# Small slot tensors in PSUM, two copies and one low half on VectorE, one low half in two steps

## The chip, the cores and the metric

The kernel runs on one core of one Trainium2 chip. The metric is device time in microseconds of one execution; of the kernel before there are three timed runs, with a median of 481.51 us (480.97 to 481.91). A separate profiled execution gave the trace; it took 479.18 us. The engines are called PE (matrix), PEld (its weight loads), DVE or VectorE, ACT or ScalarE, POOL or GpSimd, and SP (the queue that issues most DMAs).

## The reference, cut to what matters

Attention with pooled keys and values, and behind it a layer of eight experts of which each token uses one or none:

```
k_p, v_p = means of k, v over groups of 8 positions          # 576 -> 72 per head
attn_out = softmax(q @ k_p.T / sqrt(64)) @ v_p                # 8 batches, 8 heads
x = attn_out as (4608 tokens, 512)
do_compute = x @ w_skip > 0
e_idx = argmax(x[do_compute] @ w_gate);  gate = softmax weight of e_idx
out = x;  out[do_compute] += gate * (relu(xc @ w1[e]) @ w2[e])   # e = e_idx of each token
```

## The kernel before, in words

**Attention.** The 4608 tokens are 36 tiles of 128, and the loop `for t in range(NT)` takes one *turn* for each (t = 0 to 35). It is software-pipelined over three tiles. A turn records, among others, in this order: ScalarE copies the turned probabilities of tile t-2 out of PSUM (`pT`), gathers the ends of the last probabilities (`el`), and, in the turn in which a batch begins, copies its turned values (`vT`, in `turned_v`); VectorE normalises tile t-3 (`rc`, `l`, `x`, every third turn or so `lg` as well); PE computes the scores of tile t, VectorE their row minima (`mn`), PE the gate products of a new batch out of `vT`, ScalarE the exponentials (`e`); PE multiplies probabilities with values for tile t-2 (`o<-vb`, `o<-vl`) and turns the probabilities of tile t-1 (`pt<-cfs,e`, `pt<-cfs,el`). Each engine works its instructions strictly in the order in which they were recorded. The PSUM tile `pt` holds two banks; the turned values use part of the second bank, and so does the tail of the turned probabilities. `o` has one buffer of two banks, so the products of tile t-2 wait until VectorE has read those of tile t-3.

**Side work.** Lists (`act`, `dve`, `gps`) hold small jobs with a first and a last turn and are emptied by budget: key sums on VectorE, high halves of the first expert's weights on ScalarE (`high`), and on POOL the sums of values, the indirect writes of the routing table (`table<-pay`), and the low halves of the weights (`low`, weight minus its high half). `later_low` gives POOL its low halves, with the turns of `LOWS`.

**Slots.** Behind the last tile, `slots` turns the token counts into work units: a chain of some fifty VectorE steps on 128x8 tensors, most of which wait for the one before; at its middle `s_col` feeds a PE product (L1072) and `s_coli` an indirect gather by POOL (L1066) that reads rows of the table. Meanwhile PE works at the first expert on the 256 tokens that were picked early (`products`). Then a barrier, and `experts` runs the units; from there PE is busy to the end.

The names that the change touches: `TURNED`, `BESIDE`, `HALVED` are new tables; `turned_v` (L246), `low` (L607), `later_low` (L699), the end of `attention` (L978 to L1000) and the tensors at the head of `slots` (L1010 to L1024).

Of the kernel before, what the change touches and what calls it, by code (L numbers as in the profile page):

```python
# [40 lines left out]
NT = NTOK // 128  # L41
NE, F = 8, 1024
# [116 lines left out]
def attention(tc, nc, q, k, vm, vr, cf, wg, w1, w2, whi, wlo, out, c, pay, offs, table, near, bufs, late, early, mb, fin, cfs):  # L159
    with ExitStack() as ctx:  # L160
# [84 lines left out]

        def turned_v(b, tp):  # L246
            vTs[b] = vT = vp.tile([128, 3, 128], F32, name="vT", bufs=1)
            nc.scalar.activation(vT, tp, AF.Copy)

        def values_in(b, gs=slice(0, 4), by=None):  # L250
            (by or nc.gpsimd.tensor_copy)(vb[b % 2][:, gs, 0:HD], vss[b].rearrange("p (g d) -> p g d", d=HD)[:, gs])
# [343 lines left out]
        def room(cc):  # L595
            return 5 + cc % 3 if cc < 6 else cc - 6
# [4 lines left out]
        def piece(w, cc, i):  # L601
            return w[0][:, cc, i * 512:i * 512 + 512] if cc < 4 else w[1][:, (cc - 4) * 2 + i, :]
# [1 line left out]
        def high(cc, i):  # L604
            nc.scalar.activation(piece(whi, cc, i), stage[:, room(cc), i * 512:i * 512 + 512], AF.Copy)

        def low(cc, i, by=nc.gpsimd):  # L607
            return by.tensor_tensor(piece(wlo, cc, i), stage[:, room(cc), i * 512:i * 512 + 512],
                                    piece(whi, cc, i).bitcast(F32), ALU.subtract)

        def spin(o, times, n):
            for _ in range(times):
# [86 lines left out]
        def later_low(cc, i):  # L699
            if cc * 2 + i > 12:  # L700
                rest.append(lambda v: low(cc, i, v))
            else:
                ready, last = LOWS[min(cc * 2 + i - 6, len(LOWS) - 1)] if cc > 2 else (now["t"] + 1, wload(cc + 3) - 1)
                gps.add(ready, last,
                        1.25, lambda: low(cc, i))

        def adds(b, ready, last):
            first, small = sums(b)
# [269 lines left out]
        late_lows = rest[:2]  # L978
        rest[:2] = []

        def banks():
            o = ps_o.tile([128, 2, 512], F32, name="o")
            products(clock["dve"] + LATER)
            return (y.rearrange("p (i n) -> p i n", i=4) for y in (o[:, 0], ps_s.tile([128, 512], F32, name="sc")))

        fin["hot"] = (flat(kbd[0])[:, 0:PLACED * 128].rearrange("p (j n) -> p j n", j=PLACED),
                      flat(kbd[1])[:, 0:PLACED * 2 * SLOTS].rearrange("p (j i n) -> p j i n", j=PLACED, i=2))
        fin["pos"], fin["pay"] = cfs[:, 128:256], pay[:, NT - PLACED:]
        for wait in slots(tc, nc, c, offs, table, near, bufs, out, fin, ap, banks):
            if wait == "":  # L990
                products(NT * 99.0, 16)
                evacuate()
                busy[0] = False
            elif wait == "lows":
                while waiting:
                    evacuate()
                products(NT * 99.0, 11)
            elif wait == "rows":
                for f in late_lows:
                    f(nc.vector)  # L1000
            elif wait:
# [5 lines left out]
        return held, steps, rest  # L1007


def slots(tc, nc, c, offs, table, near, bufs, out, fin, p, psum):  # L1010

    rows, slot, gate, nti = (fin[n] for n in ("rows", "slot", "gate", "nti"))
    new = lambda name, dt=F32: p.tile([128, NE], dt, name="s_" + name)
    n = new("n"); ni = new("ni", I32); half = new("half", I32); odd = new("odd", I32); units = new("units")
    three = new("three", I32); wide = new("wide", I32); end = new("end"); zero = new("zero"); le = new("le")
    le1 = new("le1"); w = new("w"); more = new("more")
    none = new("none"); kind = new("kind"); own = p.tile([128, NE, NE], F32, name="s_own")
    few = p.tile([128, 1], F32, name="s_few")
    ends, short = new("ends"), new("short")
    both = p.tile([128, 2], F32, name="s_both")  # L1020
    col = p.tile([128, 4], F32, name="s_col")
    coli = p.tile([128, 1], I32, name="s_coli")
    nc.vector.memset(zero, 0.0)
    nc.vector.tensor_tensor(n, offs, c["below"], ALU.subtract)  # L1024
    yield
# [26 lines left out]
    nc.vector.tensor_tensor(w, w, le, ALU.mult)  # L1052
    yield
    nc.vector.tensor_tensor(le, le1, more, ALU.mult)
    nc.vector.tensor_reduce(col[:, 1:2], w, axis=AX.X, op=ALU.add)
    yield
    nc.vector.tensor_reduce(col[:, 0:1], le, axis=AX.X, op=ALU.add)
    nc.vector.tensor_tensor(col[:, 1:2], col[:, 1:2], near["place"], ALU.add)
    yield
    nc.vector.tensor_tensor(col[:, 0:1], col[:, 0:1], c["third"], ALU.add)  # L1060
    yield
    nc.vector.tensor_scalar(col[:, 2:3], col[:, 0:1], 1.0, float(2 * NE * JT), ALU.is_lt, ALU.mult)
    nc.vector.tensor_tensor(col[:, 1:2], col[:, 0:1], col[:, 1:2], ALU.add)
    yield
    nc.vector.tensor_tensor(coli, col[:, 1:2], col[:, 2:3], ALU.add)
# [3 lines left out]
    nc.vector.tensor_tensor(col[:, 3:4], col[:, 1:2], col[:, 2:3], ALU.add)  # L1069
    tp, tr = psum()  # L1070
    of_row = tr[:, 0, 0:SLOTS]
    nc.tensor.matmul(of_row, col[:SLOTS, 3:4].broadcast_to([SLOTS, 128]), c["ident"][:SLOTS, :SLOTS], start=True, stop=True)  # L1072
    yield ""
    at = p.tile([128, 2, PLACED], I32, name="s_at")
    atf = p.tile([128, 2, PLACED], F32, name="s_atf")
# [651 lines left out]
```

## Time and profile before

| what | us |
|---|---|
| median of three runs | 481.51 |
| the profiled execution | 479.18 |
| its span, first to last instruction | 477.3 |
| PE busy / PEld busy | 457.7 / 398.6 |
| VectorE busy | 284.0 |
| ScalarE busy | 234.2 |
| POOL busy | 206.1 |

The busy time of an engine is the time in which it worked at instructions; matrix products overlap, so a PE that is busy need not be at its peak. The span has three parts that read differently: the attention turns to about 136 us, the slot stage to about 167 us, and the expert units behind it. In rows of the timeline the columns are start, duration, engine, line, operation, out<-in with shapes, and count; brackets hold the idle time before a row and what ended it.

### The profile page before, as it was taken

The numbers are of one execution on the slowest core, as the hardware profiler recorded it, in microseconds if no ns is written. First come the engines' busy times: TensorE is split into PE (matmuls) and PEld (weight loads), VectorE is DVE, ScalarE is ACT, GpSimd is POOL, SyncE is SP. The second block draws the span as 40 slices with busy tenths as digits, with TensorE's granted clock in tenths as the row PEclk, the third lists the DMA queues.
The fourth block names the chain that finished last, engine by engine and source line by source line (L and its number), as shares of the span: only waits on it lengthen the run. The fifth ranks groups of instructions, "written<-read, shape, count | busy, mean of one in ns | idle before, by whom it ended". The sixth has DMA issues, their size and how long they took to land. (4 is left out here: it accounts for less than half of the span.)

```text
span 477.3 us, 12494 instructions
## 1 busy us (share of the span) xinstructions
PE 457.7 (96%) x4244; PEld 398.6 (83%) x4245; DVE 284.0 (60%) x659; ACT 234.2 (49%) x614; POOL 206.1 (43%) x271
## 2 busy tenths in 40 slices
PE   8999999998998899999999999999999999999993
PEld 7777777776887698989989898989898989899872
DVE  3678998988889335584746665232326532545662
ACT  4788899999861124463615443121115522434440
POOL 5588379989886330333223034422223322022020
PEclk9999999999999999999999999999999999999997
DMA  8999899966620293575754725112115542324110
GB/s 297 400 402 402 318 379 412 397 211 205 239 70 13 75 313 143 203 253 178 223 192 161 254 97 181 50 38 68 39 63 169 192 132 65 113 107 147 66 44 8
DMA packets 33216, 87.34 MB, mean 183 GB/s; under 512 B 6750, under 2 KB 7262, under 8 KB 31248
## 3 DMA queue, kind: packets, MB, share of 16 engines
q1 hardware_dynamic: 25728, 71.74, 41.9%
q0 software_dynamic: 7440, 14.99, 9.3%
q8 instruction: 27, 0.44, 0.4%
q14 instruction: 21, 0.17, 0.1%
HBM read 72.58 MB, written 20.19 MB: 194 GB/s over the span
## 5 line engine op out<-in xcount | busy, mean ns | idle before, releaser
L1382 PE MATMUL psl<-xhi,w1hi 128*128 128x256 f32 (+3 forms) x352 | 103.5, 294 | 0.3 <-PEq L1157 0.3
L1383 PE MATMUL psl<-xlo,w1hi 128*128 128x256 f32 (+3 forms) x352 | 103.4, 294 | 0.0
L1384 PE MATMUL psl<-xhi,w1lo 128*128 128x256 f32 (+3 forms) x352 | 103.4, 294 | 0.0
L1288 POOL DMA_INDIRECT out<-ring,slot x34 | 36.7, 1080 | 148.6 <-POOLq L1157 136.2
L1507 ACT ACTIVATE hhi<-psl 128x256 fp32r<-128x256 f32 (+3 forms) x88 | 36.3, 412 | 110.5 <-ACTq L1157 109.8
L1580 DVE SCALAR_TENSOR_TENSOR hlo<-psl,hhi 128x256 fp32r<-128x256 f32 (+1 forms) x88 | 38.1, 435 | 59.1 <-DVEq L1157 59.1
L301 ACT ACTIVATE e<-sc,mn 128x72 f32<-128x72 f32 x288 | 65.1, 343 | 9.9 <-DVE mn L296 9.5
L1382 PEld LDWEIGHTS psl<-xhi,w1hi 128*128 128x128 f32 x352 | 66.1, 188 | 1.1 <-issue 0.7
L1383 PEld LDWEIGHTS psl<-xlo,w1hi 128*128 128x128 f32 x352 | 66.1, 188 | 0.4
L1384 PEld LDWEIGHTS psl<-xhi,w1lo 128*128 128x128 f32 x352 | 66.1, 188 | 0.0
L1497 ACT ACTIVATE xhi<-psd 128x512 fp32r<-128x512 f32 x36 | 19.1, 599 | 73.2 <-ACTq L1157 73.2
L1283 POOL DMA_INDIRECT ring<-out,slot x36 | 41.2, 1145 | 19.1 <-issue 14.9
L1557 DVE TENSOR_TENSOR w2lo<-stage,w2hi 128x1024 fp32r<-128x1024 f32 x28 | 34.2, 1225 | 9.5 <-DVEq L1157 9.5
L410 POOL DMA_INDIRECT table<-pay,r_di x33 | 33.1, 1003 | 14.1 <-DVE p_two L437 7.6
L1404 PE MATMUL psf<-w2hi,hhi 128*128 128x512 f32 x96 | 38.1, 397 | 0.0
L1405 PE MATMUL psf<-w2lo,hhi 128*128 128x512 f32 x96 | 37.5, 390 | 0.0
L1406 PE MATMUL psf<-w2hi,hlo 128*128 128x512 f32 x96 | 37.4, 390 | 0.0
L296 DVE TENSOR_REDUCE mn<-sc 128x4 f32<-128x288 f32 x72 | 30.7, 453 | 11.2 <-PE sc L288 7.2
L1282 POOL COPY ring<-gate 128x1 f32<-128x1 f32 x33 | 8.2, 249 | 63.2 <-DMA out<-ring,slot 55.6
L1557 DVE TENSOR_TENSOR w1lo<-stage,w1hi 128x1024 fp32r<-128x1024 f32 x28 | 32.4, 1220 | 3.4 <-DVEq L1157 3.3
L1405 PE MATMUL mb<-w2lo,hhi 128*128 128x512 f32 x88 | 34.3, 390 | 0.0
L1404 PE MATMUL mb<-w2hi,hhi 128*128 128x512 f32 x88 | 34.3, 390 | 0.0
(293 smaller groups left out, 963.5 us busy)
## 6 DMA issues: line engine op xcount, KB each, us to landing
stage<-in_w SPq DMA_DIRECT2D x64, 512.0 KB, 4.7
out<-x SPq DMA_DIRECT2D x36, 256.0 KB, 7.0
stage<-in_k SPq DMA_DIRECT2D x7, 1152.0 KB
qt<-in_q SPq DMA_DIRECT2D x9, 512.0 KB, 9.9
hlo<-in_vm SPq DMA_DIRECT2D x4, 1024.0 KB, 9.0
hhi<-in_vm SPq DMA_DIRECT2D x4, 1024.0 KB
xhi<-in_q SPq DMA_DIRECT2D x4, 512.0 KB, 7.9
xlo<-in_q SPq DMA_DIRECT2D x4, 512.0 KB, 8.0
```

The lines of the kernel that those rows point to most:

```text
L301: nc.scalar.activation(e[:, g, hh * SP:(hh + 1) * SP], sc[:, h * SP:(h + 1) * SP], AF.Exp, bias=mn[:, 4 * i + h:4 * i + h + 1], scale=-1.0)
L1283: g.indirect_dma_start(ring[:, s % 6, 0:D], None, out, bass.IndirectOffsetOnAxis(ap=slot[:, s:s + 1], axis=0), bounds_check=NTOK - 1, oob_ ...
L1288: g.indirect_dma_start(out, bass.IndirectOffsetOnAxis(ap=offsets, axis=0), ring[:, s % 6, 0:D], None, bounds_check=NTOK - 1, oob_is_err=Fa ...
L1382: t.matmul(ps, whi[0][:, k, w], xhi[:, k, xs], start=(k == 0), stop=False)
L1383: t.matmul(ps, whi[0][:, k, w], xlo[:, k, xs], start=False, stop=False)
L1384: last = t.matmul(ps, wlo[0][:, k, w], xhi[:, k, xs], start=False, stop=(k == 3))
L1404: t.matmul(ps, hhi[:, k, sl], whi[1][:, k, :], start=(k == 0), stop=False)
L1405: t.matmul(ps, hhi[:, k, sl], wlo[1][:, k, :], start=False, stop=False)
L1406: last = t.matmul(ps, hlo[:, k, sl], whi[1][:, k, :], start=False, stop=(k == 7))
L1507: a.activation(hhi[:, f, xs], psL[f % 3][:, xs], AF.Relu).then_inc(sem["act"], 1)
L1557: v.tensor_tensor(chunk_of(wlo, c), chunk_view(stage[c], c), chunk_of(whi, c).bitcast(F32), ALU.subtract).then_inc(sem["wlo"], 1)
L1580: return v.scalar_tensor_tensor(out[:, f, :], psL[f % 3][:, xs], 0.0, hhi[:, f, xs].bitcast(F32), ALU.max, ALU.subtract)
```

## The change

Four edits.

1. Most small tensors of `slots` become columns of a bank of PSUM: `o[:, 1]`, the second bank of the attention's output tile, which is taken before `slots` begins. `zero`, `own`, `le`, `more`, `odd`, `wide` and a few others stay in SBUF; each step then has one SBUF tensor among its inputs at most.
2. `turned_v` copies the turned values of batches 4 and 6 with VectorE, of the others with ScalarE as before. These two copies stand in turns 18 and 27 of the loop's counter (PE turned the values at the end of turns 17 and 26).
3. The low half (4, 0), one of the 128x512 steps on `w2lo`, goes from POOL to VectorE, in turn 32 (`NT - 4`).
4. POOL makes the low half (5, 1) in two steps of 256 columns.

```
+TURNED = 4, 6
+BESIDE = 4, 0, NT - 4
+HALVED = 5, 1
...
         def turned_v(b, tp):
             vTs[b] = vT = vp.tile([128, 3, 128], F32, name="vT", bufs=1)
-            nc.scalar.activation(vT, tp, AF.Copy)
+            if b in TURNED:
+                nc.vector.tensor_copy(vT, tp)
+            else:
+                nc.scalar.activation(vT, tp, AF.Copy)
...
         def later_low(cc, i):
             if cc * 2 + i > 12:
                 rest.append(lambda v: low(cc, i, v))
+            elif (cc, i) == BESIDE[:2]:
+                dve.add(BESIDE[2], BESIDE[2], 0.7, lambda: low(cc, i, nc.vector))
             else:
...
-                gps.add(ready, last,
-                        1.25, lambda: low(cc, i))
+                parts = [slice(0, 256), slice(256, 512)] if (cc, i) == HALVED else [slice(0, 512)]
+                for part in parts:
+                    gps.add(ready, last, 1.25 / len(parts), lambda part=part: low(cc, i, nc.gpsimd, part))
...
+        o = ps_o.tile([128, 2, 512], F32, name="o")
+
         def banks():
-            o = ps_o.tile([128, 2, 512], F32, name="o")
...
-        for wait in slots(tc, nc, c, offs, table, near, bufs, out, fin, ap, banks):
+        for wait in slots(tc, nc, c, offs, table, near, bufs, out, fin, ap, o[:, 1], banks):
...
+    def new(cols=NE, dt=F32):
+        y = beside[:, taken[0]:taken[0] + cols]
+        taken[0] += cols
+        return y if dt == F32 else y.bitcast(dt)
+
+    n = new(); units = new(); end = new(); le1 = new(); w = new(); none = new(); sums = new(3)
+    ni = new(dt=I32); half = new(dt=I32); three = new(dt=I32)
```

VectorE's order around the head of turn 18, before; `kp` is the last step of turn 17, `rc`, `l`, `x` normalise tile 15, `mn` are the minima of tile 18; what an instruction waits for stands in brackets:

```order
L197 TENSOR_REDUCE kp<-stage 128x72 [waits DMAHW1_49]
L344 RECIPROCAL rc<-o 128x8 [waits PE_49]
L348 TENSOR_TENSOR l_1422<-o,rc 128x2x4x9 [waits DVE_49]
L349 TENSOR_TENSOR x<-o,rc 128x2x4x64 [waits DMAHW0_49]
L296 TENSOR_REDUCE mn<-sc 128x4 [waits PE_49,Activation_49]
L296 TENSOR_REDUCE mn<-sc 128x4 [waits PE_49]
```

And the same place now:

```order
L200 TENSOR_REDUCE kp<-stage 128x72 [waits DMAHW1_49]
L252 COPY vT<-pt 128x384 [waits Activation_49]
L350 RECIPROCAL rc<-o 128x8
L354 TENSOR_TENSOR l_1422<-o,rc 128x2x4x9 [waits DVE_49]
L355 TENSOR_TENSOR x<-o,rc 128x2x4x64 [waits DMAHW0_49]
L302 TENSOR_REDUCE mn<-sc 128x4 [waits PE_49] x2
```

The copy stands ahead of tile 15's normalising, and it waits for ScalarE: the value that it waits for is that of the `pT` copy of the same turn, which reads the same bank of `pt`. In turn 27 it is the same, with `lg` between `x` and `mn`.

VectorE's order at the head of `slots`, before:

```order
L1030 TENSOR_TENSOR s_ni<-s_n,nskip 128x8 [waits DVE_49]
L1032 TENSOR_SCALAR s_half<-s_ni 128x8 [waits DVE_49]
L1033 TENSOR_SCALAR s_odd<-s_ni 128x8
L1035 TENSOR_TENSOR s_units<-s_half,s_odd 128x8 [waits DVE_49]
L1036 TENSOR_TENSOR s_three<-s_half,s_odd 128x8
L1039 TENSOR_SCALAR s_none<-s_units 128x8 [waits DVE_49]
L1040 TENSOR_SCALAR s_units<-s_units 128x8 [waits DVE_49]
L1042 SCALAR_TENSOR_TENSOR s_end<-s_units,s_zero 128x8 [waits DVE_49]
L1043 TENSOR_SCALAR s_w<-s_units 128x8
L1044 SCALAR_TENSOR_TENSOR s_more<-s_three,s_odd 128x8
L1045 SCALAR_TENSOR_TENSOR s_more<-s_none,s_more 128x8 [waits DVE_49]
```

And now (`o` is the bank that holds the small tensors; L1055 is the scan, as L1042 was):

```order
L1043 TENSOR_TENSOR o<-o,nskip 128x8 [waits DVE_49]
L1045 TENSOR_SCALAR o<-o 128x8 [waits DVE_49]
L1046 TENSOR_SCALAR s_odd<-o 128x8 [waits DVE_49]
L1048 TENSOR_TENSOR o<-o,s_odd 128x8 [waits DVE_49]
L1049 TENSOR_TENSOR o<-o,s_odd 128x8 [waits DVE_49]
L1052 TENSOR_SCALAR o<-o 128x8 [waits DVE_49]
L1053 TENSOR_SCALAR o<-o 128x8 [waits DVE_49]
L1055 SCALAR_TENSOR_TENSOR o<-o,s_zero 128x8 [waits DVE_49]
L1056 TENSOR_SCALAR o<-o 128x8 [waits DVE_49]
L1057 SCALAR_TENSOR_TENSOR s_more<-o,s_odd 128x8 [waits DVE_49]
L1058 SCALAR_TENSOR_TENSOR s_more<-o,s_more 128x8 [waits DVE_49]
```

The steps and their order are the same, but in one bank of PSUM nearly each waits for the one before it, where four of these eleven had no wait of their own.

POOL's order up to the gather of the table's rows, before:

```order
L608 TENSOR_TENSOR w2lo<-stage,w2hi 128x512 [waits Activation_49]
L410 DMA table<-pay,r_di 36864x8 [waits DMASW0_49]
L410 DMA table<-pay,r_di 36864x8 [waits DMASW1_49]
L608 TENSOR_TENSOR w2lo<-stage,w2hi 128x512 [waits DMAHW2_49,Activation_49]
L410 DMA table<-pay,r_di 36864x8 [waits DMASW2_49,DVE_49]
L410 DMA table<-pay,r_di 36864x8 [waits DMASW3_49]
L1066 DMA stage<-table,s_coli 81x1024 [waits DMASW3_49,DMASW4_49,DVE_49,Pool_49]
```

And now:

```order
L614 TENSOR_TENSOR w2lo<-stage,w2hi 128x256 [waits Activation_49]
L416 DMA table<-pay,r_di 36864x8 [waits DMASW7_49]
L416 DMA table<-pay,r_di 36864x8 [waits DMASW0_49]
L614 TENSOR_TENSOR w2lo<-stage,w2hi 128x256
L416 DMA table<-pay,r_di 36864x8 [waits DMASW1_49]
L416 DMA table<-pay,r_di 36864x8 [waits DMASW2_49,DVE_49]
L614 TENSOR_TENSOR w2lo<-stage,w2hi 128x512 [waits DMAHW2_49,Activation_49]
L416 DMA table<-pay,r_di 36864x8 [waits DMASW3_49]
L1079 DMA stage<-table,s_coli 81x1024 [waits DMASW3_49,DMASW4_49,DVE_49,Pool_49]
```

One 128x512 step of five is gone, one is two of 256, and one write of the table comes behind the last low half instead of two. PE's and SP's instructions stand in the same order as before.

## Rows read from the trace of the kernel before

**Rows 1.** Windows: length, busy PE, PEld, DVE, ACT, POOL; clock, DMA share, GB/s.
```profile
60.00:80.00 20.00, 19.43 (x374) 15.31 (x375) 17.45 (x44) 18.87 (x71) 16.66 (x23) 1.00 1.03 393
...
320.00:340.00 20.00, 20.00 (x136) 18.43 (x136) 6.02 (x12) 3.88 (x10) 5.88 (x9) 1.00 0.16 51
```

**Rows 2.** Timeline of ScalarE in turn 18: start us, duration us, instruction.
```profile
71.54 0.70 ACT L317 ACTIVATE pT<-pt 128x640 f32<-128x640 f32 x1
...
72.42 0.47 ACT L248 ACTIVATE vT<-pt 128x384 f32<-128x384 f32 x1
...
73.31 1.80 ACT L301 ACTIVATE e<-sc,mn 128x72 f32<-128x72 f32 x8
75.37 0.70 ACT L317 ACTIVATE pT<-pt 128x640 f32<-128x640 f32 x1 [0.27 <-PE pt L313]
```

**Rows 3.** Timeline of VectorE in turn 18.
```profile
70.17 0.21 DVE L344 RECIPROCAL rc<-o 128x8 f32<-128x8 f32 x1
...
70.56 0.68 DVE L349 TENSOR_TENSOR x<-o,rc 128x512 f32<-128x512 f32 x1
72.43 0.88 DVE L296 TENSOR_REDUCE mn<-sc 128x4 f32<-128x288 f32 x2 [1.19 <-PE sc L288]
```

**Rows 4.** Timeline of PE in turn 18: values of tile 16, last turned probabilities.
```profile
73.31 0.29 PE L328 MATMUL o<-vb,pT 64*64 64x74 f32 x2
...
75.06 0.27 PE L313 MATMUL pt<-cfs,el 128*128 128x128 f32 x1
```

**Rows 5.** Timeline of VectorE in turns 27 and 28.
```profile
101.36 0.53 DVE L353 TENSOR_REDUCE lg<-l 128x27 f32<-128x216 f32 x1
102.44 0.88 DVE L296 TENSOR_REDUCE mn<-sc 128x4 f32<-128x288 f32 x2 [0.54 <-PE sc L288]
103.65 0.20 DVE L264 COPY vb<-mb 128x36 f32<-128x36 f32 x1 [0.34 <-PE mb L261]
...
106.61 0.81 DVE L296 TENSOR_REDUCE mn<-sc 128x4 f32<-128x288 f32 x2
```

**Rows 6.** Timeline of ScalarE in turns 27 and 28.
```profile
101.55 0.71 ACT L317 ACTIVATE pT<-pt 128x640 f32<-128x640 f32 x1
...
107.09 1.80 ACT L301 ACTIVATE e<-sc,mn 128x72 f32<-128x72 f32 x8 [0.24 <-DVE mn L296]
```

**Rows 7.** Timeline of PE, then of ScalarE, around the head of turn 31.
```profile
115.57 0.44 PE L242 MATMUL pt<-cfs,vs 128*128 128x128 f32 x2 [0.40 <-POOL vs L219]
...
116.21 0.70 ACT L317 ACTIVATE pT<-pt 128x640 f32<-128x640 f32 x1 [0.27 <-PE pt L243]
```

**Rows 8.** Timeline of VectorE, then of POOL, in turn 32.
```profile
122.23 0.21 DVE L344 RECIPROCAL rc<-o 128x8 f32<-128x8 f32 x1 [0.75 <-PE o L330]
...
122.97 1.28 POOL L608 TENSOR_TENSOR w1lo<-stage,w1hi 128x512 fp32r<-128x512 f32 x1
```

**Rows 9.** Timeline of VectorE, of PE and of POOL in the slot chain.
```profile
141.76 0.17 DVE L1024 TENSOR_TENSOR s_n<-offs,cfs 128x8 f32<-128x8 f32 x1
...
143.71 1.99 DVE L1042 TENSOR_TENSOR_SCAN s_end<-s_units,s_zero 128x8 f32<-128x8 f32 x1
...
147.58 0.15 DVE L1069 TENSOR_TENSOR s_col<-s_col 128x1 f32<-128x1 f32 x1
...
147.87 0.42 PE L1072 MATMUL sc<-cfs,s_col 81*128 81x81 f32 x2 [1.29 <-DVE s_col L1069]
...
144.35 1.30 POOL L608 TENSOR_TENSOR w2lo<-stage,w2hi 128x512 fp32r<-128x512 f32 x1
```

**Rows 10.** Timeline of VectorE in turn 30: dependent steps, the first into PSUM.
```profile
114.97 0.16 DVE L481 COPY mb<-p_last 128x1 f32<-128x1 f32 x1
115.17 0.17 DVE L483 TENSOR_SCALAR norder<-mb 128x8 int32<-128x8 f32 x1
```

**Rows 11.** Windows of one microsecond in the slot stage.
```profile
152.00:153.00 1.00, 1.00 (x6) 0.82 (x5) 0.96 (x9) 0.00 (x0) 1.00 (x3) 1.00 0.30 33
```

**Rows 12.** Timeline of POOL: the gather of the table's rows.
```profile
150.25 1.07 POOL L1066 DMA_INDIRECT stage<-table,s_coli x1 [2.15 <-DVE kbd L1083]
```

More of the change, by code (lines that the diff above doesn't have):

```diff
@@ L605, in high, with low @@
             nc.scalar.activation(piece(whi, cc, i), stage[:, room(cc), i * 512:i * 512 + 512], AF.Copy)
-        def low(cc, i, by=nc.gpsimd):
-            return by.tensor_tensor(piece(wlo, cc, i), stage[:, room(cc), i * 512:i * 512 + 512],
-                                    piece(whi, cc, i).bitcast(F32), ALU.subtract)
+        def low(cc, i, by=nc.gpsimd, part=slice(0, 512)):
+            return by.tensor_tensor(piece(wlo, cc, i)[:, part], stage[:, room(cc), i * 512:i * 512 + 512][:, part],
+                                    piece(whi, cc, i)[:, part].bitcast(F32), ALU.subtract)
         def spin(o, times, n):
@@ L1007, in attention, with slots @@
         return held, steps, rest
-def slots(tc, nc, c, offs, table, near, bufs, out, fin, p, psum):
+def slots(tc, nc, c, offs, table, near, bufs, out, fin, p, beside, psum):
     rows, slot, gate, nti = (fin[n] for n in ("rows", "slot", "gate", "nti"))
[L1013 to L1022, printed above, removed]
+    taken = [0]
+    def new(cols=NE, dt=F32):
[4 more added lines that the diff above has]
+    ni = new(dt=I32); half = new(dt=I32); three = new(dt=I32)
+    kept = lambda name, dt=F32, *size: p.tile([128, *(size or (NE,))], dt, name="s_" + name)
+    own = kept("own", F32, NE, NE); zero = kept("zero"); le = kept("le"); more = kept("more"); kind = kept("kind")
+    ends = kept("ends"); short = kept("short"); few = kept("few", F32, 1); odd = kept("odd", I32); wide = kept("wide", I32)
+    both = kept("both", F32, 2); col = kept("col", F32, 3); coli = kept("coli", I32, 1)
     nc.vector.memset(zero, 0.0)
@@ L1054, in slots @@
     nc.vector.tensor_tensor(le, le1, more, ALU.mult)
-    nc.vector.tensor_reduce(col[:, 1:2], w, axis=AX.X, op=ALU.add)
+    nc.vector.tensor_reduce(sums[:, 1:2], w, axis=AX.X, op=ALU.add)
     yield
-    nc.vector.tensor_reduce(col[:, 0:1], le, axis=AX.X, op=ALU.add)
-    nc.vector.tensor_tensor(col[:, 1:2], col[:, 1:2], near["place"], ALU.add)
+    nc.vector.tensor_reduce(sums[:, 0:1], le, axis=AX.X, op=ALU.add)
+    nc.vector.tensor_tensor(col[:, 0:1], sums[:, 1:2], near["place"], ALU.add)
     yield
-    nc.vector.tensor_tensor(col[:, 0:1], col[:, 0:1], c["third"], ALU.add)
+    nc.vector.tensor_tensor(sums[:, 0:1], sums[:, 0:1], c["third"], ALU.add)
     yield
-    nc.vector.tensor_scalar(col[:, 2:3], col[:, 0:1], 1.0, float(2 * NE * JT), ALU.is_lt, ALU.mult)
-    nc.vector.tensor_tensor(col[:, 1:2], col[:, 0:1], col[:, 1:2], ALU.add)
+    nc.vector.tensor_scalar(col[:, 1:2], sums[:, 0:1], 1.0, float(2 * NE * JT), ALU.is_lt, ALU.mult)
+    nc.vector.tensor_tensor(sums[:, 2:3], sums[:, 0:1], col[:, 0:1], ALU.add)
     yield
-    nc.vector.tensor_tensor(coli, col[:, 1:2], col[:, 2:3], ALU.add)
+    nc.vector.tensor_tensor(coli, sums[:, 2:3], col[:, 1:2], ALU.add)
     nc.gpsimd.indirect_dma_start(rows, None, table.rearrange("(r l) t -> r (l t)", l=128),
@@ L1068, in slots @@
                                  bounds_check=NE * JT - 1, oob_is_err=False)
-    nc.vector.tensor_tensor(col[:, 3:4], col[:, 1:2], col[:, 2:3], ALU.add)
+    nc.vector.tensor_tensor(col[:, 2:3], sums[:, 2:3], col[:, 1:2], ALU.add)
     tp, tr = psum()
     of_row = tr[:, 0, 0:SLOTS]
-    nc.tensor.matmul(of_row, col[:SLOTS, 3:4].broadcast_to([SLOTS, 128]), c["ident"][:SLOTS, :SLOTS], start=True, stop=True)
+    nc.tensor.matmul(of_row, col[:SLOTS, 2:3].broadcast_to([SLOTS, 128]), c["ident"][:SLOTS, :SLOTS], start=True, stop=True)
     yield ""
```

## The prediction

> **What bounds the kernel now.** I read the windows first, then the timelines of single engines where an edit lands, and in them the idle times and what ended them. The windows show two regimes [rows 1]. From about 180 us on PE is busy without a gap (20.00 of 20 us), all others far less: that part keeps its length and only moves with its start. In the attention turns no engine is full and none is free: in 20 us ScalarE works 18.87, VectorE 17.45, POOL 16.66. There the turn's chain decides: pT on ScalarE, then values and transposes on PE, then the next pT, and beside it scores, minima on VectorE, exponentials on ScalarE. What an edit is worth is read from who waits last in its turn. Between the two lies the slot stage, with VectorE's chain of small steps, for which PE waits 1.29 us once [rows 9].
>
> **The two copies on VectorE.** Removed from ScalarE: one copy of 0.47 us in each of two turns [rows 2]. Added to VectorE: the same copy, whose price I do not see. Below lies ScalarE's 0.47 for the same 384 columns, above VectorE's own step over 512 columns of PSUM, 0.68 [rows 2, 3]; I take 0.55, since a VectorE step over three quarters of those columns should take somewhat less than that. What counts more is what is queued behind it. VectorE works in order, the copy waits for the pT of its own turn, and rc, l, x and the minima stand behind it.
>
> Turn 18, before: rc started at 70.17 and x ended at 71.24, while VectorE would have waited anyway; the minima started at 72.43, as soon as the scores were there [rows 3]. Now nothing of this starts before pT ends, 71.54 + 0.70 = 72.24 [rows 2]. Copy 0.55, then the block from rc to x, 71.24 - 70.17 = 1.07: x ends at 73.86 and the minima start at about 73.8 (neighbours overlap by some hundredths), 1.4 later than before. The first of two is done after half of 0.88, so the exponentials start at 74.25 instead of 73.31, and end 1.80 later, at 76.05. On PE the values of tile 16 must wait for x, which reads the same buffer: 73.9 instead of 73.31. From their start to the end of the turned probabilities PE took 75.06 + 0.27 - 73.31 = 2.02 [rows 4], so these end at 75.9. The next pT, at 75.37 before, starts at 75.95 to 76.05: plus 0.6. What ScalarE saves is in this already, since it had waited 0.27 for PE there.
>
> Turn 27 is worse, since behind it VectorE has no slack. pT ends at 101.55 + 0.71 = 102.26 [rows 6]; copy 0.55, block 1.07, lg 0.53 [rows 5]: the minima start at about 104.3 instead of 102.44, plus 1.85. Of this 0.34 falls into VectorE's wait for PE before vb, and some 0.1 into overlaps; from 103.65 to the minima of turn 28 at 106.61 VectorE shows no idle time, so these come 1.4 later [rows 5]. The exponentials of turn 28 had waited 0.24 for just these minima [rows 6]: they come 1.4 later too.
>
> Taken up again is little: at the head of turn 31 PE waited for POOL's sums, which do not move, and ScalarE waited 0.27 for PE behind it [rows 7]. So the end of attention comes 0.6 + 1.4 - 0.3 = 1.7 us later. Bounds: 0.6 if only one of the two delays gets through, 2.1 if nothing is taken up and a copy costs 0.68.
>
> **The slot chain in PSUM.** From the first step to the last one ahead of PE's product it takes 147.58 - 141.76 = 5.82 us, of it 1.99 for one scan over 8 columns, where others of that size take 0.17 [rows 9]. The scan ends with POOL's 128x512 step, 144.35 + 1.30 = 145.65 [rows 9]; I read this as a wait for POOL. With its tensors in PSUM I set the scan at 0.2. The other steps lose. Their 26 spacings took 5.82 - 1.99 = 3.83, 0.15 on average, since several steps had no wait of their own. By the order 23 of the 26 now wait for the step before. A dependent step over a result in PSUM follows after 115.17 - 114.97 = 0.20 [rows 10]. So 23 x 0.20 and three of about 0.1, 4.9, and the scan's 0.2: 5.1, and with 0.2 for steps over 64 columns or with a pointer operand 5.3, which is 0.5 less than before. PE's wait of 1.29 covers this gain whole, so it reaches the path. Bounds: 0.9 less with a scan that costs nothing, 1.1 more with a scan that stays at 1.99 (4.9 + 1.99 = 6.9).
>
> [...]
>
> **POOL's part.** VectorE's low half in turn 32 costs it about 0.6 to 0.7 us (x of 512 columns: 0.68 [rows 3]). It stands where VectorE was idle for 0.75, waiting for PE's values [rows 8]; so covered I take it as nothing. Without the cover it is up to 0.7, and more in the second rival. POOL loses a step of 1.30 [rows 9]; the two halves cost no less than one step and at most as much again as a step, I take 0.2. Its last writes and the gather, at 150.25 before [rows 12], can come about 1.1 earlier. This gains nothing by itself: no row of PE shows a wait for the gather, and VectorE's chain, which also feeds it, comes later by now. I take 0, with bounds of -0.3 and 0.2.
>
> **Sum.** 1.7 - 0.5 + 0 + 0 = 1.2 us later, against the profiled execution 479.18 (span 477.3 and 1.88 around it) 480.4. The median of the runs shown lies 2.33 above that execution; I add the difference to the median: 481.51 + 1.2 = 482.7.
>
> **Rivals.**
>
> *The low half in turn 32 is held by POOL.* It reads two tensors of SBUF. In turn 32, shifted by 1.7, it would start at about 123.1, into POOL's step from 122.97 to 124.25 [rows 8]. If it is held until that ends, it is done at 124.9 instead of 123.7; rc, due at 122.23 + 1.7 = 123.9, comes 0.9 later, and with it x, PE's values and the following minima. Then the sum is 2.1, 483.6. For it: the scan's end with POOL's step [rows 9]. Against it: from 152 to 153 us VectorE ran nine short steps, several with two SBUF tensors, while POOL was busy for the whole microsecond [rows 11]. [...]
>
> *The copies gain.* If turns 18 and 27 were set by ScalarE's sum of work, each would shrink by the 0.47 that it gives up [rows 2]. With the slot chain, 2 x 0.47 + 0.5 = 1.4 less: 480.1. It decides if the first minima are ready before ScalarE is, at 73.31 - 0.47 = 72.84 in turn 18. For it: ScalarE is the busiest engine of the turns [rows 1]. Against it: the minima cannot start before x, and x not before the copy; this needs VectorE to be out of its order.
>
> *The chain gets longer.* The scan costs 2.0 by itself, and the added waits stay: 6.9 instead of 5.82, so PSUM brings the chain nothing, and the sum is 1.7 + 1.1 = 2.8: 484.3. For it: the scan started 0.64 before POOL's step that it is said to have waited for. Against it: the end, to within 0.05 us.
>
> *Only part of the delay gets through*, for instance turn 27's alone runs into slack that I did not see between turns 28 and 35: 0.6 - 0.5 = 0.1, 481.6.
>
> **How the numbers follow.** Forecast 0.45, low half held 0.20, longer chain 0.08, partial delay 0.16, copies gain 0.11. The forecast's own range is 481.9 to 483.5, from a delay of 1.4 to 2.1 and a gain of 0.1 to 0.9. About 0.2% of 481.5, or 0.96 us, is what a measurement of this kernel can tell from no change, so the band is 480.55 to 482.47. Slower: 0.72 of the forecast, all of the second and third: 0.32 + 0.28 = 0.60. Within: the rest of the forecast and nearly all of the partial delay, 0.13 + 0.16 = 0.29. Faster: 0.11. Range: up to 484.2, just short of the longer chain, and down to 480.8, where most of the gaining case is left out.
>
> **What would show it.** In the profile after, VectorE should be idle for about 2 us ahead of vT in turns 18 and 27, with ScalarE as what ended it; the minima of these turns should start 1.4 and 1.8 us later, and the first step of the slot chain some 1.7 us later, at about 143.5. The scan should take about 0.2 us and the chain 5.3, with PE's wait at its product near 0.8. The low half in turn 32 should take 0.7 us; with 1.2 or more it was held. If the slot chain's first step comes no later than 141.8, the forecast is wrong at its first and largest term; if the scan keeps its 2 us, at its second.

## The result, and where the time went

The changed kernel is slower by 3.7 us: a median of 484.64 us over 21 runs (479.79 to 490.90), against 480.97 us over 21 runs of the kernel before on the same chips. The ratio is 1.0077, with a 95% interval of 1.0056 to 1.0098. That lies above the range of the prediction. Medians are over all executions, ratios and intervals over those that did not run in a slower state, so the two need not agree. The profiled execution took 485.65 us, its span 483.8, so it stands 6.5 us over the profiled one of before (479.18, span 477.3), and more has to be accounted for in the pair of traces than in the medians.

A ruler for the attention turns is the start of ScalarE's pT at the head of each turn, read from the timelines of the two profiles:

| head of turn | before | after | later by |
|---|---|---|---|
| 9 | 41.55 | 41.17 | -0.38 |
| 13 | 55.59 | 57.55 | +1.96 |
| 18 | 71.54 | 73.49 | +1.95 |
| 19 | 75.37 | 77.89 | +2.52 |
| 27 | 101.55 | 104.02 | +2.47 |
| 30 | 112.35 | 116.08 | +3.73 |
| 31 | 116.21 | 120.83 | +4.62 |
| 33 | 122.94 | 127.55 | +4.61 |
| 34 | 125.80 | 130.92 | +5.12 |

The start is 0.4 us earlier, and the loss comes in six pieces: 2.3 us between turns 9 and 13, 0.6 in turn 18, 1.3 from turn 27 to 30, 0.9 in turn 30, 0.5 from turn 32 (it shows between the heads of turns 33 and 34), and then 1.2 at the slots (below).

The first piece stands ahead of anything that was changed. In the timeline of PE of the profile after, two rows wait for nothing that the profile shows, in the middle of a run of matmuls:

```profile
44.08 0.42 PE L334 MATMUL o<-vb,pT 64*64 64x74 f32 x12 [0.44 <-issue]
...
52.20 0.66 PE L336 MATMUL o<-vl,pT 64*64 64x296 f32 x2 [1.44 <-issue]
```

Five kernels that lack a part of the change will show the same stall, two of them in one profile and not in another, so it is counted here as no part of the change; its cause is open. Without it the pair differs by about 4.2 us, close to the medians.

Turns 18 and 27 went as forecast. VectorE after, in turn 18 and then turn 27:

```profile
74.22 0.56 DVE L252 COPY vT<-pt 128x384 f32<-128x384 f32 x1 [2.03 <-ACT pT L323]
74.70 0.20 DVE L350 RECIPROCAL rc<-o 128x8 f32<-128x8 f32 x1
...
75.08 0.68 DVE L355 TENSOR_TENSOR x<-o,rc 128x512 f32<-128x512 f32 x1
75.68 0.81 DVE L302 TENSOR_REDUCE mn<-sc 128x4 f32<-128x288 f32 x2
...
104.75 0.56 DVE L252 COPY vT<-pt 128x384 f32<-128x384 f32 x1 [2.07 <-ACT pT L323]
...
106.66 0.82 DVE L302 TENSOR_REDUCE mn<-sc 128x4 f32<-128x288 f32 x2
```

VectorE stands still for 2 us ahead of each copy, and rc, x and the minima that had filled that time [rows 3, 5] come after it. ScalarE pays: its exponentials in turn 18 now wait 1.17 us for the minima.

```profile
76.16 1.80 ACT L307 ACTIVATE e<-sc,mn 128x72 f32<-128x72 f32 x8 [1.17 <-DVE mn L302]
77.89 0.70 ACT L323 ACTIVATE pT<-pt 128x640 f32<-128x640 f32 x1
```

The next three pieces were not forecast, or only as a rival. They are one thing in three places: a VectorE step is *held*, that is, it takes far longer than the same step elsewhere and ends only with a step of POOL. VectorE and POOL after, at turn 30, in turn 32 and at the slots' first step; then PE's two waits:

```profile
115.53 1.36 DVE L474 TENSOR_TENSOR mb<-offs,p_apart 128x8 f32<-128x8 f32 x1
...
126.02 1.43 DVE L614 TENSOR_TENSOR w2lo<-stage,w2hi 128x512 fp32r<-128x512 f32 x1
...
146.86 1.89 DVE L1037 TENSOR_TENSOR o<-offs,cfs 128x8 f32<-128x8 f32 x1
...
150.75 0.18 DVE L1055 TENSOR_TENSOR_SCAN o<-o,s_zero 128x8 f32<-128x8 f32 x1
...
153.90 0.15 DVE L1082 TENSOR_TENSOR s_col<-o,s_col 128x1 f32<-128x1 f32 x1
...
115.57 1.27 POOL L222 TENSOR_TENSOR hhi<-hhi 128x512 f32<-128x512 f32 x1
...
125.62 1.27 POOL L614 TENSOR_TENSOR w1lo<-stage,w1hi 128x512 fp32r<-128x512 f32 x1
...
147.39 1.32 POOL L614 TENSOR_TENSOR w2lo<-stage,w2hi 128x512 fp32r<-128x512 f32 x1
...
117.77 0.44 PE L334 MATMUL o<-vb,pT 64*64 64x74 f32 x13 [0.74 <-DVE p_few L476]
...
154.20 0.42 PE L1085 MATMUL sc<-cfs,s_col 81*128 81x81 f32 x2 [2.51 <-DVE s_col L1082]
```

Three VectorE steps with two inputs in SBUF are held: one ends at 116.89 where POOL's sums end at 116.84, one at 148.75 where POOL's low half ends at 148.71, and the low half at 127.45, 0.56 us after POOL's end at 126.89 (0.68 is what it takes where it is not held). The 8-column sum of offs and p_apart had taken 0.15 before. The scan, which was held before [rows 9], now takes 0.18; its hold went to the chain's first step, so the chain takes 153.90 - 146.86 = 7.04 us from its first step to its last, 5.82 before, and PE waits 2.51 in place of 1.29.

### The profile page after: what moved, and what is told of

Its sections match the earlier page's. It is cut to its first block, busy times and chain, and to the rows that moved or that the text cites. A ratio compares the mean times of both kernels' runs of the same rounds, so it can differ in the third digit from the quotient of the medians.

```text
span 483.8 us, 12491 instructions
## 1 busy us (share of the span) xinstructions
PE 458.7 (95%) x4244; PEld 398.8 (82%) x4245; DVE 287.7 (59%) x662; ACT 233.1 (48%) x612; POOL 203.6 (42%) x271
## 5 line engine op out<-in xcount | busy, mean ns | idle before, releaser
L1301 POOL DMA_INDIRECT out<-ring,slot x34 | 35.5, 1045 | 153.1 <-POOLq L1170 140.9
L1419 PE MATMUL mb<-w2hi,hlo 128*128 128x512 f32 x88 | 34.3, 390 | 0.0
```

Of the source, the lines that this page charges most:

```text
L1301: g.indirect_dma_start(out, bass.IndirectOffsetOnAxis(ap=offsets, axis=0), ring[:, s % 6, 0:D], None, bounds_check=NTOK - 1, oob_is_err=Fa ...
L1419: last = t.matmul(ps, hlo[:, k, sl], whi[1][:, k, :], start=False, stop=(k == 7))
```

## Experiments

Theory A: a copy that must wait for pT stops VectorE in order, so VectorE slips against POOL; and a VectorE step with two SBUF inputs is held wherever it meets a POOL step of that kind. Theory B, in its several forms: each edit costs by itself. The expectations give its form for each run. Ratios are to the kernel before, run on the same chip, with 95% intervals; 0.0021 is 1 us.

**One part at a time.** First the copies alone:

```diff
+            if b in TURNED:
+                nc.vector.tensor_copy(vT, tp)
+            else:
                 nc.scalar.activation(vT, tp, AF.Copy)
```

> The kernel before with only the two copies of turned values on VectorE (batches 4 and 6). Theory A (VectorE waits in order for its own turn's pT, and the turns behind it slip into a POOL step): VectorE stands idle about 2 us ahead of each of the two copies; the step from pT to pT grows by 0.6 us in turn 18 and by 1.2 us in turns 27 and 28, and in turn 30 the small product of offs and p_apart takes about 1.3 us in place of 0.15, because it now falls beside POOL's 512-column sums, for another 0.9 us; the slots' chain keeps its 5.8 us. Sum +2.7: about 483.7 us. Theory B (the copies cost next to nothing and the loss is that of the slots and the low half): within 0.3 us of the kernel before, 481.0 us, pT to pT unchanged in both turns.

Measured: 481.33 us, ratio 1.0032 (0.9990 to 1.0074); in the profile the end of attention comes 2.5 us later than before, 2.8 counted from the first turn. Turn 18 grows by 0.57, turns 27 to 29 by 1.25, turn 30 by 1.1. Its rows of VectorE, POOL and PE in turn 30:

```profile
113.25 1.56 DVE L472 TENSOR_TENSOR mb<-offs,p_apart 128x8 f32<-128x8 f32 x1
...
113.50 1.27 POOL L220 TENSOR_TENSOR hhi<-hhi 128x512 f32<-128x512 f32 x1
...
115.69 0.75 PE L332 MATMUL o<-vb,pT 64*64 64x74 f32 x32 [0.95 <-DVE p_few L474]
```

By the trace A's 2.7 us was right to 0.1. The times alone allow -0.5 to 3.6 us. So the hold in turn 30 follows from the copies; it is not in the code that was changed. At the slots the first step was held (1.90) in place of the scan (0.18), with all tensors in SBUF: the chain took 5.7 us and PE waited 1.19, no more than before.

Then the slots' tensors alone, the changed kernel with its other two parts switched off:

```diff
-TURNED = 4, 6
-BESIDE = 4, 0, NT - 4
-HALVED = 5, 1
+TURNED = ()
+BESIDE = 99, 0, NT - 4
+HALVED = 99, 1
```

> The kernel before with only the slots' small tensors in PSUM. Theory A: POOL's 512-column step stands 2.6 us behind the chain's first step as before, where every step now has at most one SBUF input, so the scan takes 0.2 us and no other step is held; the chain is 5.3 us (5.8 before), PE waits 0.8 us in place of 1.3, time -0.5 us: about 480.5 us. Theory B (small steps in PSUM are themselves slower, or are held all the same): the chain is 6.5 to 7 us, PE waits 2 to 2.5 us, about 482.2 us.

Measured: 479.68 us, ratio 0.9980 (0.9941 to 1.0018). The chain is 5.3 us, the scan 0.18, PE's wait 0.78: A, and the forecast's own term of -0.5. The first step stood 2.5 us ahead of POOL's step and took 0.17. By itself this part does what it should; B, slower by 1 us or more, is excluded.

The low halves alone, the kernel before with the changed later_low and low:

```diff
+BESIDE = 4, 0, NT - 4
+HALVED = 5, 1
```

> The kernel before with only the low half of turn 32 on VectorE and the other one made in two steps. Theory A: the low half falls into VectorE's idle time beside POOL's descriptor writing and takes 0.7 us, nothing is late behind it; POOL's last 512-column step now stands 0.5 us behind the chain's first step in place of 2.6, so the first step of the chain (two SBUF inputs) takes 1.9 us and the scan 0.2: the chain stays at 5.8 us and the time within 0.3 us of 481.0 us. Theory B (the low half on VectorE is held by POOL wherever it stands): it takes 1.4 us and the time is +0.5 to +0.9 us, about 481.7 us.

Measured: 484.43 us, ratio 1.0048 (0.9997 to 1.0100), too wide to tell. The profiled run took 478.97. In it the low half took 0.73 beside a DMA_INDIRECT of POOL of 1.03 us (the expectation calls it descriptor writing), and nothing was late behind it. My expectation for the chain was wrong: POOL's last low half stayed 2.5 us behind the first step (144.22 against 141.69), and the scan was held again (2.00). So POOL's new order by itself does not bring the two together: in the changed kernel the first step comes 5.2 us later than here, POOL's step only 3.2. A second profile of this kernel:

> The kernel with only the low halves moved, once more, for a second profile, since half of its times lay near 485 us. Theory A: the scan or another step of the slots' chain is held for some 1.8 us as before, the low half takes 0.7 us, and what is longer than the kernel before is a stall of PE that the profile gives no reason for. Theory B: the low half or the chain is held for 1 us or more beyond that.

It took 487.28 us with the low half at 0.68 and the scan at 2.00, and a first step held for 0.64 by POOL's half step. 4.9 us of it is one wait of PE in the experts' loop, at 220 us, long after the change, which was 0.5 in the first profile; the mean granted clock was 0.96 from 140 to 180 us, with PE's wait of 1.77 us at the slots, and 0.97 from 180 to 240, where the kernel before had 1.00 in both. The low half by itself was not held in either.

**One input of the chain's first step moved.** The changed kernel, with the constant of that step in PSUM:

```diff
+        o = ps_o.tile([128, 2, 512], F32, name="o")
+        nc.vector.tensor_copy(o[:, 1, 248:256], c["below"])
         add_routes(NT)
...
-    nc.vector.tensor_tensor(n, offs, c["below"], ALU.subtract)
+    nc.vector.tensor_tensor(n, offs, beside[:, 248:256], ALU.subtract)
```

> The changed kernel with one more edit: the constant that the chain's first step subtracts is copied into PSUM ahead of the last tiles' routes, so that this step has one SBUF input too. Theory A (the step is held for POOL's 512-column step since it has two SBUF inputs): the first step takes 0.2 us in place of 1.9, the chain 5.3 us in place of 7.0, PE's wait before the product 0.8 us in place of 2.5: -1.6 us against the changed kernel, about 483.0 us. Theory B (whatever step comes there is held, or the first step waits for something else): another step of the chain takes about 1.9 us, the chain stays at 7.0 us and the time at 484.6 us.

Measured: 483.62 us, ratio 1.0056 (1.0025 to 1.0087), where A said 483.0 and B 484.6. The time does not tell them apart: +1.2 to +4.2 us holds both, and this profile had a PE stall of 1.74 us at 102. The trace does. VectorE, POOL and PE at the slots; last, from the run *shift* below, the same VectorE step with both inputs in SBUF, and the POOL step that it met:

```profile
145.29 0.17 DVE L1037 TENSOR_TENSOR o<-offs,o 128x8 f32<-128x8 f32 x1
...
144.39 1.31 POOL L614 TENSOR_TENSOR w2lo<-stage,w2hi 128x512 fp32r<-128x512 f32 x1
...
150.90 0.42 PE L1085 MATMUL sc<-cfs,s_col 81*128 81x81 f32 x2 [0.78 <-DVE s_col L1082]
...
147.43 0.43 DVE L1030 TENSOR_TENSOR s_n<-offs,cfs 128x8 f32<-128x8 f32 x1
...
146.51 1.32 POOL L611 TENSOR_TENSOR w2lo<-stage,w2hi 128x512 fp32r<-128x512 f32 x1
```

The step starts 0.90 us into POOL's and takes 0.17; PE's wait falls from 2.51 to 0.78. In *shift* it starts 0.92 us into POOL's, and takes 0.43, to POOL's end. With one input in SBUF the step was not held here. Nor was one with two in the stretch of rows 11, in the kernel before:

```profile
152.58 0.15 DVE L1098 TENSOR_TENSOR s_none<-s_none,s_odd 128x8 f32<-128x8 f32 x1
...
151.38 1.90 POOL L1081 TENSOR_SCALAR kbd<-cfs,s_atf 128x128 f32<-128x128 f32 x3
```

There a VectorE step with two SBUF tensors took 0.15 us beside POOL's steps of one SBUF tensor with a scalar. So, one misfit below apart, only POOL's two-tensor steps are seen to hold in the traces read here.

**The copies in another place.** The copies alone, each behind the normalising:

```diff
-            if new:
+            if new and new not in TURNED:
                 turned_v(new, tp)
             if t > 2:
                 normal(t - 3)
+            if new in TURNED:
+                turned_v(new, tp)
```

> The kernel with only the two copies on VectorE, and there each stands behind the normalising of three turns before in place of ahead of it. Theory A (the loss in turns 18 and 27 is VectorE standing still, in order, behind a copy that has to wait for pT): VectorE does rc, l and x in those 2 us, the minima are late by 0.6 us at most, the step from pT to pT grows by at most 0.3 us in turn 18 and 0.4 us in turns 27 and 28 together (0.6 and 1.2 with the copy ahead). The slip at turn 30 is then under 1 us, and the small product of offs and p_apart is held less or not at all. About +0.5 us against the kernel before: 480.7 us by its 480.2 us of the last comparison. Theory B (a copy out of this bank on VectorE costs its time wherever it stands): the growth of 0.6 and 1.2 us stays, about 482 us.

Measured: 479.50 us, ratio 0.9989 (0.9959 to 1.0018). VectorE in turn 18, then the product of turn 30:

```profile
71.94 0.21 DVE L348 RECIPROCAL rc<-o 128x8 f32<-128x8 f32 x1
...
72.33 0.68 DVE L353 TENSOR_TENSOR x<-o,rc 128x512 f32<-128x512 f32 x1
...
74.04 0.56 DVE L250 COPY vT<-pt 128x384 f32<-128x384 f32 x1 [1.02 <-ACT pT L321]
74.51 0.81 DVE L300 TENSOR_REDUCE mn<-sc 128x4 f32<-128x288 f32 x2
...
113.45 0.15 DVE L472 TENSOR_TENSOR mb<-offs,p_apart 128x8 f32<-128x8 f32 x1
```

The same copy of 0.56 us now costs nothing: turns 18 and 27 are each 0.06 us shorter than before. The place cost the 1.8 us, not the copy. The changed kernel with this one edit:

> The changed kernel with one more edit: in turns 18 and 27 the copy on VectorE stands behind the normalising of three turns before. Theory A (the copies' place makes VectorE slip, and the slip makes it meet POOL in turns 30 and 32 and at the slots' first step): pT to pT grows by 0 to 0.1 us in turns 18, 27 and 28, the product of offs and p_apart takes 0.15 us, the low half 0.7 us; POOL's 512-column step again stands some 2.5 us behind the chain's first step, which takes 0.2 us, so the chain is 5.4 us and PE waits 0.8 us. Time -0.5 us against the kernel before: about 479.6 us by its 480.0 us. Theory B (the slots' tensors or the low half lose by themselves): only 1.8 us of the loss goes, about 482.5 us.

Measured: 480.24 us, ratio 0.9980 (0.9955 to 1.0004). The product takes 0.15, the low half 0.68. B is excluded. One number was off: POOL's half step fell on the first step (0.64 in place of 0.2), so the chain was 5.8 and PE's wait 1.2.

**A slip with no copy on VectorE.** The low halves moved, and ScalarE copies vT several times in turn 18, five in the first run and four in the later ones:

```diff
-            nc.scalar.activation(vT, tp, AF.Copy)
+            for _ in range(5 if b == 4 else 1):
+                nc.scalar.activation(vT, tp, AF.Copy)
```

> The kernel with only the low halves moved, and a delay with no other purpose: in turn 18 ScalarE copies the turned values five times in place of once, some 2.1 us. No copy is on VectorE and no slot tensor in PSUM. Theory A (what was lost in turns 30 and 32 and at the slots' first step comes from VectorE slipping against POOL, whose steps do not slip with it): besides the 2.1 us, the small product of offs and p_apart takes 1 to 1.6 us in place of 0.15 and PE waits 0.7 to 0.9 us behind it; the low half on VectorE in turn 32 takes 1.2 to 1.5 us in place of 0.73; one step of the slots' chain is held as before, an early one in place of the scan. Sum 3.2 to 3.8 us, about 484 us. Theory B (those holds belong to the copies and to the tensors in PSUM): only the 2.1 us, the product stays at 0.15 us and the low half at 0.73, about 482.3 us.

Measured: 488.18 us, ratio 1.0131 (1.0075 to 1.0187), and both theories' numbers failed. Turn 18 grew by 3.6 us, not 2.1: PE waited 2.21 for vT and then ran at a lower clock, as the windows of three microseconds show (the third number from the end is the granted clock, 1.00 for the full one):

```profile
71.00:74.00 3.00, 1.25 (x8) 1.03 (x8) 0.89 (x3) 2.87 (x7) 2.80 (x4) 1.00 1.05 416
74.00:77.00 3.00, 2.22 (x52) 1.69 (x52) 0.96 (x3) 2.90 (x11) 2.92 (x6) 0.72 1.06 421
77.00:80.00 3.00, 3.00 (x33) 2.47 (x33) 1.66 (x5) 1.25 (x3) 2.82 (x3) 0.71 0.97 396
80.00:83.00 3.00, 3.00 (x76) 2.40 (x72) 2.88 (x8) 3.00 (x13) 2.72 (x4) 1.00 1.03 353
```

A PE stall without a reason (1.47 us at 105) came on top. VectorE was carried past POOL's steps: the product met only POOL's 256-column sum (0.75 us), the low half none (0.68), and the slots' chain took 4.3 us, so PE did not wait for it. The other large piece of this profile is a wait of PE in the experts' loop, 4.65 us at 222 (0.38 before). Hence the smaller delay:

> As the run with the delay, but with four copies of the turned values by ScalarE in turn 18 in place of five, so that VectorE reaches turn 30 some 1.6 us later (three copies more of 0.52 us) and not 5 us. Still no copy on VectorE and no slot tensor in PSUM. Theory A (a VectorE step with two inputs in SBUF waits wherever it meets a POOL step of 512 columns, and the slip decides which meet): the product of offs and p_apart now starts within 0.6 us of POOL's sums and takes 1.0 to 1.6 us, PE waits 0.7 to 0.9 us behind it, and the low half in turn 32 starts inside POOL's low half and takes 1.2 to 1.5 us, for 0.5 us more: +3 us in all, 482.8 us by 480 us of the kernel before. Theory B (POOL slips along, or the holds belong to the edits themselves): 0.15 and 0.7 us for the two steps, and +1.6 us, 481.6 us.

Measured: 483.93 us, ratio 1.0087 (1.0056 to 1.0119), that is +4.2 us (2.7 to 5.7), where A said 3 and B 1.6. Turn 18 grew by 1.57, as worked out. But the profiled run had the stall at 105 again, besides the one at 44 and 52, and showed 0.80 and 0.68 us, so its time is no evidence for A. Two more profiles (single executions of 486.38 and 484.09 us):

> The kernel with the delay of 1.6 us once more. Theory A: where PE has no stall between turns 18 and 30, the product of offs and p_apart starts within 0.6 us of POOL's 512-column sums and takes 1.0 to 1.6 us in place of 0.15, and the low half in turn 32 starts inside POOL's low half and takes 1.0 to 1.5 us in place of 0.7; where PE has such a stall again, both start later than those POOL steps and are held only by what POOL does then. Theory B: 0.15 and 0.7 us though VectorE stands beside those POOL steps.

> The same kernel and the same expectations as the run before it, for a second profile in case a stall of PE falls between turns 18 and 30 again.

In the first VectorE's product started 0.72 us ahead of POOL's 512-column sums, 0.04 ahead of a 256-column one, and took 0.16, the low half 0.68; with a slip of 1.6 us the meeting had been missed by a little. In the second turns 18 and 19 slipped by 4.5 together, with PE's granted clock at 0.70, 0.50 and 0.67 from 72 to 81 us, and it happened, in a kernel with nothing on VectorE or in PSUM but the low half:

```profile
115.31 1.67 DVE L471 TENSOR_TENSOR mb<-offs,p_apart 128x8 f32<-128x8 f32 x1
...
126.12 0.91 DVE L611 TENSOR_TENSOR w2lo<-stage,w2hi 128x512 fp32r<-128x512 f32 x1
...
146.47 1.85 DVE L1030 TENSOR_TENSOR s_n<-offs,cfs 128x8 f32<-128x8 f32 x1
...
115.67 1.27 POOL L221 TENSOR_TENSOR hhi<-hhi 128x512 f32<-128x512 f32 x1
...
125.18 1.29 POOL L611 TENSOR_TENSOR w1lo<-stage,w1hi 128x512 fp32r<-128x512 f32 x1
...
146.99 1.31 POOL L611 TENSOR_TENSOR w2lo<-stage,w2hi 128x512 fp32r<-128x512 f32 x1
```

All three holds of the changed kernel are there. At the slots this costs nothing here: the chain is 5.7 us, PE waits 1.15. Read over all eighteen profiles, the product's duration goes with its start relative to that of POOL's 512-column sums: 0.15 to 0.16 us in the nine that start 1.36 to 1.88 ahead (the kernel before among them); 0.16 at 0.72 ahead; 1.36 to 1.67 in the four from 0.36 to 0.04 ahead; 0.75 to 0.80 in the three that start 1.6 behind, on the 256-column sum. One does not fit: 0.72 at 1.32 ahead.

**POOL kept off the chain.** The low halves moved, and at the end POOL's last low halves ahead of its last table writes; slots in SBUF, copies on ScalarE:

```diff
-                        i = work if self.wrote > (t > NT - 7) or work[0] < write[0] and work[0] <= t else write
+                        i = work if t > NT or self.wrote > (t > NT - 7) or work[0] < write[0] and work[0] <= t else write
...
         pts[NT - 1] = turned_p()
-        gps.take(NT + 99)
```

> The kernel with only the low halves moved, and POOL's last low halves ahead of its last table writes in place of between them, so that no POOL step of 512 columns falls on the slots' chain; all slot tensors in SBUF. Theory A (the chain is 5.8 us long only because one step of it is held): no step takes more than 0.4 us, the chain is 4.0 us, PE's wait before the product goes from 1.3 us to 0 to 0.2, and all that follows comes 1.2 us earlier: about 479.0 us by the 480.2 us of the kernel before. Theory B (another step is held, or the late table writes hold the gather): the chain stays near 5.8 us, or the gather starts later than 2 us behind the chain's end; no gain.

Measured: 478.41 us, ratio 0.9949 (0.9923 to 0.9975): faster than the kernel before, by 2.5 us (1.2 to 3.7). The first profile, of an execution of 484.66 us, has a wait of PE of 4.34 us in the experts' loop again. A second profile:

> The kernel with POOL's last low halves ahead of its last table writes once more, for a second profile. Theory A: the slots' chain is 4.1 us with no step over 0.4 us, PE's wait before the product under 0.2 us, the low half in turn 32 takes 0.7 us; span 476 us, or 478 us where PE has its stall early in the run. Theory B: the chain's length of 4.1 us was chance, one of its steps takes over 1 us here.

It took 479.98 us, with 1.6 us of PE stall early. VectorE, POOL and PE at the slots, then VectorE and POOL in turn 30:

```profile
143.81 0.18 DVE L1028 TENSOR_TENSOR s_n<-offs,cfs 128x8 f32<-128x8 f32 x1
...
145.63 0.17 DVE L1046 TENSOR_TENSOR_SCAN s_end<-s_units,s_zero 128x8 f32<-128x8 f32 x1
...
147.83 0.15 DVE L1073 TENSOR_TENSOR s_col<-s_col 128x1 f32<-128x1 f32 x1
...
138.34 2.70 POOL L610 TENSOR_TENSOR w2lo<-stage,w2hi 128x256 fp32r<-128x256 f32 x3
...
148.47 0.35 PE L1076 MATMUL sc<-cfs,s_col 81*128 81x81 f32 x2
...
113.58 0.72 DVE L470 TENSOR_TENSOR mb<-offs,p_apart 128x8 f32<-128x8 f32 x1
...
113.19 0.99 POOL L412 DMA_INDIRECT table<-pay,r_di  x1 [0.17 <-issue]
```

The chain is 4.0 us, no step is held, PE does not wait for it: 1.3 us of the gain; the rest was not traced. The product of turn 30 is the misfit above: 0.72 us, to 0.12 us behind the end of POOL's DMA_INDIRECT. The same order with the slots in PSUM, and then in SBUF with the late copies:

> As the run with POOL's last low halves ahead of its last table writes, with the slots' small tensors in PSUM besides. Theory A (steps that share one PSUM tile follow each other at 0.21 us each, where many in SBUF follow at 0.08): no step is held, yet the chain is 5.3 to 5.5 us, so 1.3 to 1.5 us longer than with the tensors in SBUF; PE waits 0.8 us; about 479.9 us. Theory B (PSUM costs the chain nothing once POOL is away): chain 4.0 us, as with SBUF, about 479.0 us.

> The best of the parts so far: the kernel before with the low half of turn 32 on VectorE, POOL's last low halves ahead of its last table writes, the slots' tensors in SBUF, and the two copies on VectorE behind the normalising. Theory A: no step of the slots' chain is held, the chain is 4.1 us, PE's wait before the product under 0.2 us, and the copies gain 0.1 us in each of their turns: about 478.4 us by 480.0 us of the kernel before, as the run with the low halves first, or 0.2 us under it. Theory B (the two edits meet each other): the slip moves another step onto POOL's, no gain over the kernel before.

Measured: 480.51 us, ratio 0.9989 (0.9953 to 1.0025), chain 5.3 us, PE's wait 0.79; and 479.19 us, ratio 0.9970 (0.9929 to 1.0011), chain 4.3, no wait. With POOL away, PSUM makes the chain 1.3 us longer. That is the loss of 1.2 at the slots of the changed kernel: with the slots in SBUF a hold on the first step leaves the chain at 5.7, as one on the scan does; with the 1.3 on top it is 7.0. The late copies add nothing.

**The changed kernel again.**

> The changed kernel once more, beside the others on one chip. Theory A: VectorE again stands idle 2 us ahead of each of its two copies; what happens from turn 30 on depends on where it meets POOL, so the product of offs and p_apart and the slots' first step are held in this profile if PE's stall of 1 to 2 us early in the run (which waits for nothing that the profile shows) is there or not there alike, since POOL slips with that one; +3 to +4.5 us, 483 to 484.5 us. Theory B (the stall early in the run belongs to the changed kernel): it is there again at 44 and 51 us, and is at least 1.4 us of the difference.

Measured: 487.27 us over six runs, ratio 1.0134 (1.0082 to 1.0186). VectorE idle 2.04 and 2.08 us ahead of the copies, the product 1.56, the low half 0.97, the first step 1.85, PE's wait 2.5. The time is above A's 483 to 484.5. In the profile, PE's granted clock was 0.68 and 0.75 over the six microseconds from 153, behind the wait at the slots, and 1.8 us more were lost from there to 221 us, where the first profile lost 0.2. The stall at 44 and 51 us was there, 1.05 us of it; it was there too in profiles of five kernels that lack one change or more (the late copies alone, the delay and the low halves first among them), so it does not need the change; how often it comes in each kernel is not known.

## Why the prediction was wrong

The direction was right, the size was not: forecast 1.2 us, measured 3.7 (2.7 to 4.7).

- *The copies.* The step held. VectorE idle 2.03 and 2.07 where 2 was forecast, 0.57 for 0.6 in turn 18, 1.26 for 1.4 in turn 27; the copy 0.56 for 0.55.
- *"Taken up again is little", -0.3.* Wrong in sign: +0.9. I asked what the slip would run into on PE, not on POOL; VectorE's product of offs and p_apart had stood 1.36 us ahead of POOL's sums and now fell on them. The copies-only run shows it.
- *"The slot chain in PSUM", -0.5.* This is the step that failed most: +1.2. Its spacing was right (5.3 forecast, 5.3 measured when nothing was held), and so was the scan's 0.2. But I took the hold as the scan's own and not as that of whatever two-input step stands there. The first step still read offs and a constant from SBUF, though the account of the change gives every step one SBUF input at most, and POOL's 512-column step came 0.5 us behind the first step's start in place of 2.6. Both rows were in view [rows 9]; where POOL's step would stand after the slip I did not work out.
- *The low half in turn 32.* Forecast 0, with a rival of +0.9: the rival happened, at +0.5 in one profile and nearly 0 in the other. What I held against it [rows 11] did not bear on it: POOL's work in that microsecond was three steps of one tensor with a scalar, none with two tensors as the low half has.
- *The chain gets longer* was the rival nearest in time, by luck: it kept 2 us on the scan, which took 0.18; that another step was held instead brought its +1.1 near the +1.2.
- *The copies gain* had a wrong reading in its favour: ScalarE's 18.87 us of 20 [rows 1] are less than PE's 19.43. The copies did not gain, as the forecast had it.

The terms as measured, 0.57 + 1.26 + 0.9 + 0.5 + 1.2, make 4.4 in the one profile; the medians say 3.7. How often each meeting happens from run to run, and how often PE's clock falls behind a wait, stays open.

## What to carry to other kernels

Before an edit lets one engine slip, list the steps on it that can be held by another engine, and ask which pairs the slip brings together; a hold can change its place in a chain (1.99 us on the scan before, 1.89 on the first step after). A copy that must wait belongs behind the work that need not (ahead of it, the two copies cost 0.57 and 1.26 us, behind it nothing). Moving the holder out of the chain's way left PE no wait, making the chain's steps immune to it left 0.78 us.

## What the runs showed of the hardware

- In the meetings above, POOL's two-tensor steps held VectorE's two-SBUF-input steps to their end, within 0.05 us for the short ones (0.43 to 2.00 us in place of 0.15 to 0.18). In nine steps of the slots' chain the hold began 0.49 to 0.65 us ahead of the POOL step's own row, while POOL's row before, a DMA_INDIRECT of 0.98 to 0.99 us, ran. Not every such step was held: one product began 0.04 us ahead of a 256-column POOL step's row and took 0.16. Whether a DMA_INDIRECT holds by itself, as the one misfit of 0.72 us suggests, was not settled; six other products began 0.11 to 0.35 us into such a row and took 0.15.
- PE stalled in the attention turns without a shown reason in ten of the eighteen profiles, always inside the values' matmuls and near the same places: for 1.1 to 2.4 us at 44 and 52 us, or for 1.5 to 1.7 at 102 to 105, once at both. The cause is open; it is as large as most effects looked for here.
- One wait of PE in the experts' loop, at 213 to 222 us, took 4.3 to 5.3 us in four of the eighteen profiles (*low_first*, *low_only_b*, *shift*, *shift_less_b*) and at most 0.9 in the others, among them other profiles of three of these kernels. In each of the four the granted clock was low beside it, 0.50 to 0.69 in the lowest three microseconds. The cause is open.
- The same wait of PE was followed by a lower clock in one profile and not in another. The changed kernel's wait at the slots was followed by 1.00 in one profile (2.51 us) and by 0.68 and 0.75 over six microseconds in the other (2.47 us). The wait for vT in turn 18 with the smaller delay, 1.70 us in all three profiles, was followed by 1.00 in two, and in the third by 0.50 over three microseconds. After the 2.21 us of the larger delay the mean was 0.72 and 0.71 over six.
